# Chunk-sparse attention and softplus MLP on one core: paired casting loads, a causal triangle on TensorE, wide zero matmuls and a new order

## The chip, the cores and the metric

The kernel runs on one core of one Trainium2 chip. The metric is the device time of one launch in microseconds. The kernel before takes 265.45 us (median of three runs, 265.19 to 266.56).

## The reference

Attention over 4 batches, 8 heads, 768 positions and head size 64, then a two-layer MLP with softplus. Each query may look at its 6 best chunks of 32 keys, ranked by an upper bound from the chunk's element-wise minimum and maximum of k; the causal mask goes on top.

```python
k_min, k_max = k_chunks.min(axis=3), k_chunks.max(axis=3)      # 24 chunks of 32 keys
ub = sum(maximum(q * k_min, q * k_max))                        # [B, H, S, 24], causal by chunk
top_chunks = argsort(ub)[..., -6:]
scores = where(chosen & (pos_q >= pos_k), q @ k.T / sqrt(64), -1e9)
x = (softmax(scores) @ v) -> [B*S, H*D]                        # 3072 x 512
out = softplus(x @ w_in) @ w_out                               # 512 -> 2048 -> 512
```

## The kernel before, in words

The work is cut into 12 blocks: 4 batches times 3 blocks of 256 queries. Block n has k = n mod 3; its queries see 2(k+1) key tiles of 128. The stages of a block are these.

- **Loads.** q, k and v come in as bf16. The general loader `load` (L339) issues two casting DMAs on POOL's queue for each tensor, one for each tile of 128 tokens; every run that they write is one head of one token, 64 bf16 numbers. They go to an `io` buffer (8 of them), v to a resident tile. k and q of block 0 take another way, `load_pairs` (L352): two uncast loads for each on SP's queue, in which a partition holds two neighbouring tokens, and a cast on ScalarE (`io<-xp`, L258).
- **Turning.** In blocks 0 to 2, TensorE transposes k and q (L471, four matmuls for each tile of 128 tokens) into a PSUM tile; from block 3 on, SP's DMA transposes do it (L475). DVE takes chunk maxima and minima (`kx`, L498 and L490), puts them into a block-diagonal `bd`, and ScalarE or DVE copies k into the resident tiles `ka`, `kb` and q into `qt`, `qa`.
- **Choice.** Relu parts of q (`qpos`, `qneg`, L547 to L551) times `bd` give the bounds (L570, L574). DVE finds the sixth largest for each row (L597) and writes a mask `mraw` (L612), which is transposed (L627, L633 on TensorE, L636 by DMA) and copied beside q (`qa<-ph`, `qt<-pt`, at the copy helper's lines L258 for ScalarE and L259 for DVE). The mask then acts through extra rows of the score matmul.
- **Scores and values.** L687 and L688 make the scores of a pair of key tiles in PSUM, ScalarE takes the exponential (L695), and on the last pair of key tiles POOL zeroes what lies above the diagonal (`affine_select`, L705, in every block). L717 multiplies with v, DVE divides (L727, L728), and the result is turned into `x` (L743 on TensorE in blocks 0 to 2, L732 by DMA later).
- **MLP.** L791 makes h in 8 groups of 8 matmuls for a block, ScalarE takes exp (L796) and log(1+e) (L801) into `g`, L816 makes y, and SP stores it (L827).

The order is written by a planner at build time. `make_plan` lists operations with a duration for each engine that may run it, buffers from small pools, and a due time (`key`); `Plan.run` places them one by one by due time and by the earliest time at which its model has engine, data and buffer free, and the instructions are then issued in that order on every engine. Its model of the two DMA queues is a few lines in `run`; due times come from the numbers in `PAR`. `keep_awake` then fills every gap of over about 0.1 us that the plan leaves on TensorE before 45 us with matmuls of zeros, 128 columns wide (L852).

Of the kernel before, what the change touches and what calls it, by code (L numbers as in the profile page):

```python
# [63 lines left out]

class Op:
    __slots__ = ("name", "alts", "fn", "deps", "gate", "after", "succ", "alloc", "touch", "key",
                 "rel", "packet", "port", "due", "wait", "eng", "start", "end", "done", "dma", "n", "at", "inst")


class Plan:  # L70
# [5 lines left out]
    def op(self, name, alts, fn, deps=(), alloc=(), touch=(), key=None, dma=None, gate=(), after=(), rel=0.0, packet=19.0, port=False):  # L76
        o = Op()
        o.rel, o.packet, o.port = round(rel), packet, port
# [50 lines left out]
    @staticmethod  # L129
    def home_at(pool, s, e):  # L130
        t = 0.0
        for q, x, dma in pool.ends[s]:
            t = max(t, x + (LANDED[e] if dma else 0 if q == e == "PE" else LAT[q].get(e, 150)))
        return t

    def run(self, par):
# [7 lines left out]
        for o in reversed(topo):  # L144
            dur = min(c for _, c in o.alts) + (2500 if o.dma else 160)
            o.due = min([o.key] + [s.due - dur for s in o.succ])
        free = {"PE": 3000.0, "ACT": 2300.0, "DVE": 1000.0, "POOL": 800.0, "SP": 800.0}
        ring, packet = {"SP": 0.0, "POOL": 0.0}, {"SP": 19.0, "POOL": 32.0}
# [3 lines left out]
        while ready:  # L152
# [26 lines left out]
            if o.dma:  # L179
                other = "SP" if e == "POOL" else "POOL"  # L180
                at = max(o.end + (650 if e == "SP" else 1150), ring[e], 2650.0)
                back, part = max(0.0, ring[other] - at), packet[other] / o.packet
                ring[e] = at + o.dma + min(o.dma * part, back)
                ring[other] += min(o.dma, back / part)
                packet[e] = o.packet
                o.done = ring[e] + (450 if o.packet < 100 else 1000)
                if e == "SP":
                    o.end = max(o.end, ring[e] - 3500)
            else:
                o.done = o.end  # L190
# [4 lines left out]
            for b in o.touch:  # L195
                b.left -= 1
                b.ends.append((e, o.done, bool(o.dma)))
# [14 lines left out]
def mm(n):  # L212
    return max(25.0, n / 2.4 + 2.5)
# [6 lines left out]
def dve(n, rate=1.0):  # L220
    return n / (0.96 * rate) + 66


PAR = dict(
    dmat=3,
    dmaT=450,
    narrow=1,
    l0=1,
    over="soy",
    maskD=3,  # L230
    awake=(1.06, 45.0, 5.7),
    first=(64.42, 64.23, 29.03, 95.39),
    loads=((87.43, 130.15, 71.7), 19.14, (76.86, 12.06, 15.17), 41.22),
    tol={"PE": 0, "ACT": 0, "DVE": 0, "POOL": 2358, "SP": 0},
    alt=636,
    ohd=(229.35, 150.58),
    a=(-46.8, -33.92, -31.03, -0.05, 17.1, 24.77, 54.71, 88.7, 133.12, 175.62, 173.66, 255.42, 297.45, 469.8),
    prep=((77.31, -48.97, -81.43, 46.38), (-8.14, 24.92, -67.86, -43.68), (53.78, -16.07, -58.0, 11.26), (25.03, -41.37, -16.45, 11.23)),
    av=(-0.8, 4.76),
    ot=(12.12, 10.86),  # L240
    hlag=(8.7, 27.7, 34.1, -3.53, 34.9, 33.84, 33.54, 32.2, 25.36, -32.32, 54.03, 77.81),
    ylag=(7.32, 7.87, 25.64, 26.35, 28.67, 47.05, 47.88, 49.45, 10.02, 22.03, 47.36, 37.39),
    ahead=(3.4, 19.67, 10.64, 22.05, 12.72, 9.33, 70.63, 47.4, 103.95),
    sizes=dict(s=2, h=2, y=1, o=1, t=2, xf=2, xp=4, kT=2, io=8, kx=2, q=2, pn=2, ub=2, pt=4, osb=4, x=4, g=2, e=4, ysb=4, mT=2),
# [3 lines left out]
def make_plan(T, par):  # L248
# [19 lines left out]
    P.op("zero", [("DVE", 80)], lambda e: nc.vector.memset(T.zero, 0.0), key=-100000)  # L268
# [26 lines left out]
    chunk_rows = [P.op("c4", [("POOL", 900)], f4, [r4], key=3000)]  # L295
    mr0, bd0, kb0, vone, ohk = [], [], [], [], {}
# [11 lines left out]
    for k0, k1 in ((0, 1), (1, NBLK)):  # L308
        for h in range(2):
            o = P.op("ohk", [("SP", 450)], lambda e, k0=k0, k1=k1, h=h: rows_of(0, k0, k1, h), oh[k0:k1],  # L310
                     key=par["ohd"][k0] * 1e3, dma=300 * (k1 - k0))
# [636 lines left out]
```

## Time and profile before

| | |
|---|---|
| median of 3 runs | 265.45 us (265.19 to 266.56) |
| the profiled execution | 266.59 us, of which the span of its instructions is 264.8 us |
| TensorE busy | 255.0 us (96%), 2750 matmuls recorded |
| ScalarE, DVE, POOL busy | 211.0 us (80%), 142.5 us (54%), 110.8 us (42%) |
| DMA moved | 29.87 MB, 113 GB/s over the span |
| granted clock of TensorE, mean | 0.994 |

The busy share of TensorE holds the zero matmuls (22.7 us), and the ends of matmuls are modelled, so it has to be read with the timeline: what counts is when real matmuls start one right behind the other.

### The profile page before, as it was taken

How to read it: one execution, taken by the hardware profiler on the slowest of the kernel's cores; microseconds unless marked ns; L12 is line 12 of the kernel's file. 1: busy time of each engine (PE TensorE's matmuls, PEld its weight loads, DVE VectorE, ACT ScalarE, POOL GpSimd, SP SyncE). 2: the span in 40 equal slices, each digit the busy share in tenths (PEclk: the TensorE clock that was granted, in tenths of full speed). 3: DMA queues.
4: the chain of work that ended last, by engine and by line, in shares of the span. 5: the costliest groups of instructions: out<-in, count | busy, mean ns of one | idle time of the engine just before them, and what ended most of it. 6: DMA issues, size and time to landing. Idle time of an engine off the chain costs nothing.

```text
span 264.8 us, 7039 instructions
## 1 busy us (share of the span) xinstructions
PE 255.0 (96%) x2750; PEld 197.2 (74%) x2779; DVE 142.5 (54%) x500; ACT 211.0 (80%) x372; POOL 110.8 (42%) x193
## 2 busy tenths in 40 slices
PE   8698999999999999999999999999999999999995
PEld 8698898768775677788678864777888756887744
DVE  6589961019789667447634596584582164221012
ACT  3589999988687879999687992699997885999900
POOL 8927878798318520543990263401110211310000
PEclk9799999999999999999999999999999999999999
DMA  7996999999999984699699969624440123001022
GB/s 162 161 189 90 181 196 231 155 139 190 149 136 173 132 119 89 115 129 100 73 173 150 117 88 174 173 54 120 45 82 0 42 72 99 10 2 42 0 79 79
DMA packets 114719, 29.87 MB, mean 113 GB/s; under 512 B 104544, under 2 KB 111712, under 8 KB 114688
## 3 DMA queue, kind: packets, MB, share of 16 engines
q0 software_dynamic: 74944, 13.11, 66.5%
q1 hardware_dynamic: 39744, 16.33, 33.0%
q8 instruction: 21, 0.34, 0.6%
q14 instruction: 10, 0.08, 0.1%
HBM read 27.26 MB, written 6.29 MB: 127 GB/s over the span
## 4 chain that ended last, share of the span: by engine, by line
PE 86%; DMA 5%; DVE 3%; ACT 3%; issue 1%; POOL 0%; DVEq 0%; POOLq 0%
PE ph L791 30%; PE py L816 17%; PE pt L816 9%; PE po L717 7%; PE ps L687 5%; PE py L852 4%; PE ps L688 4%; DMA io<-in_k_dram 3%; DMA x<-osb 3%; PE pt L687 2%; PE pt L688 1%; PE pt L570 1%; ACT g L801 1%; PE ph L816 1%; ACT e L796 1%
## 5 line engine op out<-in xcount | busy, mean ns | idle before, releaser
L791 PE MATMUL ph<-x,w_in_sb 128*128 128x256 bf16 x768 | 91.8, 272 | 0.0
L705 POOL TENSOR_SCALAR_AFFINE_SELECT pt<-pt 128x256 bf16<-128x256 bf16 x96 | 39.5, 419 | 112.6 <-ACT pt L695 112.1
L791 PEld LDWEIGHTS <-w_in_sb 128*128 128x128 bf16 x768 | 73.6, 98 | 11.5 <-DMA w_in_sb<-in_moe_w_in_dram 0.5
L695 ACT ACTIVATE pt<-ps 128x512 bf16<-128x512 f32 (+1 forms) x134 | 69.9, 564 | 9.4 <-PE ps L688 8.8
L796 ACT ACTIVATE e<-ph 128x512 f32<-128x512 f32 x96 | 56.3, 606 | 12.5 <-PE ph L791 11.8
L816 PEld LDWEIGHTS <-g 128*128 128x128 bf16 x400 | 37.4, 98 | 31.4 <-ACT g L801 0.5
L816 PE MATMUL py<-w_out_sb,g 128*128 128x512 bf16 x231 | 57.8, 379 | 1.5 <-ACT ysb L258 0.2
L801 ACT ACTIVATE g<-e 128x1024 bf16<-128x1024 f32 x48 | 51.1, 1072 | 1.0
L695 ACT ACTIVATE pt<-pt 128x512 bf16<-128x512 f32 (+1 forms) x58 | 32.4, 584 | 0.6 <-PE pt L688 0.6
L717 PEld LDWEIGHTS <-pt 128*128 128x128 bf16 x672 | 26.8, 97 | 5.1 <-issue 0.6
L259 DVE COPY ysb<-py 128x512 f32<-128x512 f32 x12 | 8.3, 691 | 36.9 <-PE py L816 36.9
L717 PE MATMUL po<-v,pt 128*128 128x65 bf16 x610 | 26.4, 193 | 0.3 <-DVE osb L728 0.3
L816 PE MATMUL pt<-w_out_sb,g 128*128 128x512 bf16 x108 | 26.2, 379 | 0.2
L727 DVE RECIPROCAL rec<-po 128x4 f32<-128x4 f32 x43 | 7.6, 178 | 34.9 <-PE po L717 34.6
L490 DVE TENSOR_REDUCE kx<-kT 128x32 bf16<-128x1024 bf16 x18 | 21.0, 1209 | 8.9 <-DMA kT<-io 8.9
L852 PE MATMUL py<-zero 128*128 128x128 bf16 x243 | 22.7, 245 | 1.1 <-DVE zero L268 1.1
L339 POOL DMA_DIRECT2D v<-in_v_dram x24 | 21.6, 905 | 3.8 <-DMA io<-in_q_dram 1.5
L339 POOL DMA_DIRECT2D io<-in_k_dram x22 | 20.0, 910 | 5.7 <-DMA w_in_sb<-in_moe_w_in_dram 2.2
L339 POOL DMA_DIRECT2D io<-in_q_dram x22 | 19.9, 910 | 0.7 <-PE ph L791 0.6
L728 DVE TENSOR_TENSOR osb<-po,rec 128x256 bf16<-128x256 f32 x43 | 18.2, 424 | 2.7 <-DMA x<-osb 1.3
L852 PEld LDWEIGHTS <-zero 128*128 128x128 bf16 x243 | 18.3, 111 | 1.3 <-DVE zero L268 1.1
L687 PE MATMUL ps<-qa,ka 96*128 96x256 bf16 x71 | 18.3, 273 | 0.7 <-DVE qa L259 0.7
(99 smaller groups left out, 302.5 us busy)
## 6 DMA issues: line engine op xcount, KB each, us to landing
out_dram<-ysb SPq DMA_DIRECT2D x23, 256.0 KB, 2.4
v<-in_v_dram POOLq DMA_DIRECT2D x24, 128.0 KB, 7.6
io<-in_k_dram POOLq DMA_DIRECT2D x22, 128.0 KB, 7.2
io<-in_q_dram POOLq DMA_DIRECT2D x22, 128.0 KB, 7.1
w_out_sb<-in_moe_w_out_dram POOLq DMA_DIRECT2D x4, 512.0 KB, 8.0
w_in_sb<-in_moe_w_in_dram POOLq DMA_DIRECT2D x4, 512.0 KB, 9.6
xp<-in_k_dram SPq DMA_DIRECT2D x2, 256.0 KB, 3.2
xp<-in_q_dram SPq DMA_DIRECT2D x2, 256.0 KB, 6.3
```

Of the source, the lines that this page charges most:

```text
L339: lambda e, t=t: nc.gpsimd.dma_start(out=into(nm, n, t), in_=rows(nm, n, t)),
L490: nc.vector.tensor_reduce(kx.ap[:, :, j].rearrange("d p (t c) -> d t p c", t=NT), kT.ap.rearrange("d p x -> d (p x)").rearrange("d (t p c ...
L687: nc.tensor.matmul(sp.ap[:, 0:QB], kk[0:nr, p, j * 128:(j + 1) * 128], qq, start=True, stop=True)
L695: lambda e, sp=sp, pt=pt, h=h, j=j, w=w: nc.scalar.activation(pt.ap[:, h, j:j + 2].rearrange("k j c -> k (j c)")[:, 0:w], sp.ap[:, 0:w], A ...
L705: nc.gpsimd.affine_select(out=d, in_=d, compare_op=ALU.is_ge, fill=0.0, base=0, channel_multiplier=-1, pattern=[[0, 2], [1, 128]])
L717: nc.tensor.matmul(o[:, u, h], pt.ap[:, h, j, c0:c0 + 128], T.V[i][:, j, 2 * p + h, :], start=(j == 0), stop=(j == t0 + u))
L728: nc.vector.tensor_tensor(osb.ap[0], o[:, :, :, 0:D], osb.ap[1].to_broadcast([128, NT, 2, D]), op=ALU.mult)
L791: nc.tensor.matmul(o[:, j], T.w_in[:, dt, ft * 128:(ft + 1) * 128], x.ap[:, dt], start=(dt == 0), stop=(dt == KDM - 1))
L796: lambda e, hb=hb, eb=eb, f2=f2: nc.scalar.activation(eb.ap[:, f2 * 512:(f2 + 1) * 512], hb.ap, ACT.Exp),
L801: lambda e, eb=eb, g=g, f4=f4: nc.scalar.activation(g.ap[:, f4 * 4:(f4 + 1) * 4].rearrange("f j c -> f (j c)"), eb.ap, ACT.Ln, bias=1.0),
L816: nc.tensor.matmul(yb.ap[:, 0:c1 - c0], g.ap[:, f, u * 128:(u + 1) * 128], T.w_out[:, f, c0:c1], start=(f == 0), stop=(f == KFF - 1))
L852: z.fn = lambda e: T.nc.tensor.matmul(T.pools["y"].homes[0][:, 0:128], T.zero, T.zero, start=True, stop=True)
```

## The change

1. `load_both`: q of block 0 and k, q of blocks 1 and 2 come in as one casting DMA each on POOL's queue, in which a partition holds two neighbouring tokens and every run that is written is 128 bf16 numbers, where before it was two DMAs with runs of 64 (and, for q of block 0, two uncast loads on SP's queue and two casts on ScalarE). Since a pair of tokens then lies between the heads, TensorE turns each head by itself: 16 transposes of 64 columns for a tensor in place of 8 of 128. k of block 0 stays as it was.
2. In blocks 0 to 2 the causal triangle is added to the scores by a matmul of the identity with a triangle of large negative numbers, two for each last pair of key tiles, and POOL's `affine_select` on the exponentials falls away there. From block 3 on it stays.
3. Zero matmuls are up to 512 columns wide.
4. The planner gets a finer model of the two DMA queues (`Rings`), other costs of transfers, other due times and an offset for each name of an operation (`tweak`), and other pool sizes: `io` 4 for 8, `kT` 3 for 2, `pt` 5 for 4, `osb` 3 for 4, `e` 3 for 4. So the order on every engine is new.

```diff
+    def both(x):
+        return x.rearrange("s t h d -> s (t h d)").rearrange("s (h t d) -> s h t d", h=H, t=NT)
+
+    def load_both(nm, n, when):
+        b, k = blocks[n]
+        SBt[nm, n] = Buf(pool["io"])
+        o = P.op(f"ld {nm}{n}", [("POOL", 900)], lambda e: nc.gpsimd.dma_start(
+            out=both(SBt[nm, n].ap), in_=src[nm][b, :, k * QB:(k + 1) * QB].rearrange("h (s t) d -> s h t d", t=NT)),
+                 key=1e3 * when, dma=1280, packet=20.0, land=SKEW, alloc=[SBt[nm, n]])
...
             def transposes(nm, buf, t, n=n, ps=ps, p0=p0, whole=whole):
                 o = t_of(buf)
                 for p in ps:
+                    if whole[nm]:
+                        for h in range(2):
+                            nc.tensor.transpose(o[h * 64:(h + 1) * 64, p - p0, t * 128:(t + 1) * 128],
+                                                both(SBt[nm, n].ap)[:, 2 * p + h, t], T.ident)
+                        continue
...
-                        nc.tensor.matmul(sp.ap[:, 0:QB], kk[0:nr, p, j * 128:(j + 1) * 128], qq, start=True, stop=True)
-                        nc.tensor.matmul(sp.ap[:, QB:w], kk[0:nr, p, (j + 1) * 128:(j + 2) * 128],
-                                         qq[:, 1] if last else qq, start=True, stop=True)
+                        add = last and tri
+                        for c0, c1, x in ((0, QB, qq), (QB, w, qq[:, 1] if last else qq)):
+                            jj = j + c0 // QB
+                            nc.tensor.matmul(sp.ap[:, c0:c1], kk[0:nr, p, jj * 128:(jj + 1) * 128], x, start=True, stop=not add)
+                            if add:
+                                nc.tensor.matmul(sp.ap[:, c0:c0 + 128], T.ident, T.tri, start=False, stop=True)
...
-                    if last:
+                    if last and not tri:
                         def f_a(e, pt=pt, h=h, t0=t0):
...
-    l0=1,
+    l0=2,
+    both=3,
+    tri=3,
...
-    sizes=dict(s=2, h=2, y=1, o=1, t=2, xf=2, xp=4, kT=2, io=8, kx=2, q=2, pn=2, ub=2, pt=4, osb=4, x=4, g=2, e=4, ysb=4, mT=2),
+    sizes=dict(s=2, h=2, y=1, o=1, t=2, xf=2, xp=4, kT=3, io=4, kx=2, q=2, pn=2, ub=2, pt=5, osb=3, x=4, g=2, e=3, ysb=4, mT=2),
...
-        while True:
-            c = 107 if t < 1e3 * par["awake"][2] else mm(128)
...
+        for w in (512, 128):
+            while True:
+                c = w / 1.2 if t < 1e3 * par["awake"][2] else mm(w)
+                if t + c > o.start - 60:
+                    break
...
+                z.fn = lambda e, w=w: T.nc.tensor.matmul(T.pools["y"].homes[0][:, 0:w], T.zero[:, 0:128], T.zero[:, 0:w],
+                                                         start=True, stop=True)
```

Counted in the built programs: the zero matmuls go from 243 (all 128 wide) to 49 (33 of 512 and 16 of 128); the transposes of k and q from 48 to 88; 48 triangle matmuls are new; the selects on POOL go from 96 to 72; POOL's loads of q and k from 44 to 41. All other matmuls are as many as before.

200 lines of the change are left out of this document (133 added, 67 removed).

## The prediction

> **What bounds the kernel now.** I read the page first, for who is busy when.
>
> ```profile
> span 264.8 us, 7039 instructions
> ...
> PE   8698999999999999999999999999999999999995
> ...
> ACT  3589999988687879999687992699997885999900
> ...
> PEclk9799999999999999999999999999999999999999
> ...
> L705 POOL TENSOR_SCALAR_AFFINE_SELECT pt<-pt 128x256 bf16<-128x256 bf16 x96 | 39.5, 419 | 112.6 <-ACT pt L695 112.1
> ```
>
> TensorE's digits say 90% and more nearly everywhere, but zeros count as busy. So next came the busy time by stretch, of the zero matmuls alone and of all, and TensorE's timeline for the first real matmul of an MLP.
>
> ```profile
> 0.00:10.00 10.00, 5.80 (x52) 5.36 (x53) 0.11 (x1) 1.00 1.28 161
> 10.00:20.00 10.00, 7.33 (x79) 5.76 (x78) 0.00 (x0) 0.83 1.79 180
> 20.00:30.00 10.00, 5.85 (x79) 4.68 (x78) 0.00 (x0) 1.00 0.93 119
> ```
> ```profile
> sum 225.50, PE 223.49 PEld 167.98 DVE 112.77 ACT 183.52 POOL 83.45; mean PE 55.87 PEld 42.00 DVE 28.19 ACT 45.88 POOL 20.86
> ```
> ```profile
> 36.06 1.03 PE L791 MATMUL ph<-x,w_in_sb 128*128 128x256 bf16 x8
> ```
>
> The first three rows (time, busy us of zeros, count, ..., clock, DMA) show TensorE mostly on zeros for 30 us. The sum row covers 36.0 to 261.5 us: busy 223.5 of 225.5. So there are two kernels: a start-up until the first h at 36.06 us, bound by a chain of handoffs, and a rest bound by TensorE's own work. For that work I take start-to-start times from the chain of waits.
>
> ```profile
> 2.08 7.38 DMA io<-in_k_dram
> ...
> 10.12 2.22 PE py L852 x23
> ...
> 19.25 0.78 PE py L852 x14
> ...
> 43.19 2.62 PE ph L791 x24
> ...
> 60.33 0.66 PE po L717 x22
> ...
> 73.14 0.86 PE py L816 x4
> ```
>
> That is 109 ns for a matmul 256 wide, 215 for 512, 30 for 65 (values), 56 for 128 (14 in 0.78). Times the counts, with 26 ns for the small bounds matmuls (an estimate below the 30), the real matmuls are 234.2 us before and 239.1 after; the difference is 40 more transposes and 48 triangles, 88 x 56 ns = 4.9 us. In the instruction orders 11.5 us of that stand ahead of the first h before, 11.4 after. So before, 222.7 us of work after the first h take 225.5 us: 2.8 us are lost there, all the rest in the start-up.
>
> **What the change adds.** On TensorE 227.7 us are left after the first h instead of 222.7: 5.0 us dearer, on the path. Everything then hangs on how much sooner the first h comes. The zeros cost nothing while real work waits for its inputs: 33 wide and 16 narrow ones at 215 and 56 ns are 8.0 us, against 13.6 for 243 narrow ones; where one runs over, the next real matmul is late by 0.2 us at most.
>
> **The start-up, step by step.** Rows of ScalarE, DVE and POOL:
>
> ```profile
> 4.72 0.62 ACT L258 CAST io<-xp 128x512 bf16<-128x512 f32 x1 [0.26 <-DMA xp<-in_k_dram]
> ...
> 10.16 0.59 ACT L258 COPY qt<-ph 128x512 bf16<-128x512 bf16 x1 [0.80 <-PE ph L471]
> 10.64 0.62 ACT L258 CAST io<-xp 128x512 bf16<-128x512 f32 x1
> ...
> 16.30 1.06 ACT L547 ACTIVATE qpos<-qt 128x1024 bf16<-128x1024 bf16 x1
> 17.41 0.57 ACT L258 COPY qa<-ph 32x512 bf16<-32x512 bf16 x1
> ...
> 21.44 0.87 ACT L695 ACTIVATE pt<-ps 128x384 bf16<-128x384 f32 x2
> 22.20 1.00 ACT L258 COPY ka<-pt 64x1024 bf16<-64x1024 bf16 x1
> ...
> 27.09 0.50 ACT L695 ACTIVATE pt<-ps 128x384 bf16<-128x384 f32 x1
> ...
> 29.13 5.62 ACT L695 ACTIVATE pt<-ps 128x512 bf16<-128x512 f32 x11
> 34.64 0.64 ACT L258 COPY x<-pt 128x256 bf16<-128x256 bf16 x2
> ```
> ```profile
> 5.33 2.48 DVE L498 TENSOR_REDUCE kx<-pt 128x16 bf16<-128x512 bf16 x4 [0.80 <-PE pt L471]
> 7.73 1.17 DVE L259 COPY bd<-kx 64x32 bf16<-64x32 bf16 x2
> ...
> 10.98 0.66 DVE L549 TENSOR_SCALAR qneg<-qt 128x512 bf16<-128x512 bf16 x1
> 11.56 0.34 DVE L259 COPY bd<-kx 64x32 bf16<-64x32 bf16 x2
> ...
> 16.43 1.21 DVE L498 TENSOR_REDUCE kx<-ph 128x32 bf16<-128x1024 bf16 x1
> ...
> 31.84 0.42 DVE L728 TENSOR_TENSOR osb<-po,rec 128x256 bf16<-128x256 f32 x1
> ```
> ```profile
> DMA packets 3638, 0.47 MB, mean 156 GB/s; under 512 B 3616, under 2 KB 3638, under 8 KB 3638
> ```
> ```profile
> DMA packets 1135, 1.13 MB, mean 188 GB/s; under 512 B 33, under 2 KB 1135, under 8 KB 1135
> ```
>
> *q of block 0.* No row shows a casting load with runs of 256 B. Its rate lies between the loads with runs of 128 B alone (first row above, 8 to 11 us, 156 GB/s) and the weights, runs of 1 KB (second, 32 to 38 us, 188 GB/s): 256 KB take 1.4 to 1.7 us; I take 1.4 for its size beside 1.7 for two loads now, 0.3 us a tensor. It is POOL's first DMA, at about 1.7 us. The first pair of loads there, issued at 2.08, took 7.38 us to reach TensorE, beside four loads on SP's queue; two of those go. If nothing is saved it lands at 1.7 + 7.38 = 9.1; with half the traffic beside it and a shorter transfer I take 7.4 or before, all the same to TensorE, which is busy until 7.4: k's second cast ends at 5.34, and behind it stand transposes and zeros of 22 x 128 columns, 2.1 us at 2.22/23 = 97 ns each. So the load is hidden; if it lands at 9.1, all below is 1.7 us later. ScalarE is rid of two casts of 0.62, POOL's queue of one issue a tensor, and q of block 0 now stands ahead of k of block 1 there, which moves k's transposes behind q's.
>
> The Trainium skill (DMA: Bandwidth & Descriptors, Anatomy of one DMA) gives each DMA about 2 us fixed plus its bytes at 436 GB/s; by that a merged load saves 2 us a tensor, 10 us for five. The trace disagrees for queued loads: two in a row stream at 156 GB/s without such a gap. The sum keeps 0.3.
>
> *Mask of block 0.* 16 transposes of q take 0.9 us (7.4 to 8.3), two copies of 0.59 each to 9.5. DVE reduces k (2.48) with four `bd` copies between (1.17 and 0.34) until 9.3, then two `qa` copies and four relus, six at 0.5 (between `bd`'s 0.17 and 0.66), to 12.3; bounds, maxima and compares, 0.7 by small DVE pieces of 0.17, to 13.0. TensorE has 16 transposes of k of block 1 queued before the mask's transposes: to 13.9. The first mask copy starts at 14.1, against 17.41 before. The 3.3 us come from q's second half, which before was cast only at 10.64 and turned behind other work, and from half the clock: 23 zeros took 2.22 us where 14 later took 0.78.
>
> *Exponentials.* From that copy to the last exponential of block 0, ScalarE has, by the new order, four mask copies of 0.57 and two of like size, a relu of 1.06, k's two copies of 1.00, eight exponentials of 0.44 and a small copy of 0.33: 10.4 us, to 24.5. Before, the same point is 27.59. Lead 3.1 us. The new wait, scores for `tri`, is made on POOL behind the loads of q, k, v and one of w_out by about 14; the first scores come at 15.6, and if `tri` were late the whole chain would be.
>
> *First h.* Before, the way from 27.6 to 36.06 went over the selects on POOL, eleven exponentials of block 1 (29.13 to 34.75) and then ScalarE's copies of `x` at 34.64. The 24 selects of blocks 0 to 2 go, 0.42 us each, and values wait for ScalarE alone; nothing on POOL now holds up loads behind a select there. After: values 0.3, division 0.6, a reduction of k of block 2 ahead on DVE 1.21, the transposes and a copy 0.5: 27.2, and TensorE's order lets it through at 27.4. Weights: w_in's first quarter is in the first 2.5 MB on POOL's queue, 13 to 16 us of transfer from 4 us on at the two rates, landed by 24. Lead 8.7 us.
>
> *After it.* 27.4 + 227.7 + the same 2.8 lost = 257.9 against 261.5: gain 3.6 us. ScalarE must keep up: from 24.5 its order holds 28 exponentials at 0.51 (5.62 for 11), 11 of L796 of the same size, five of L801 at 1.0 like a copy of as many columns and 1.7 of copies, 26.6 us to 51.1; TensorE's 23.6 us to the values that wait for them end at 51.0 too. Level, so some of each will wait for the other; I leave the loss as it was and take **3.5 us**. The profiled execution took 266.6, 1.8 us outside its 264.8 span; it stands 1.1 above the median, from which I subtract: 265.45 - 3.5 = 262.0. Own range 260 to 264.
>
> **Rivals.**
>
> *More: the added 5 us hide (chance 0.14).* If ScalarE, not TensorE, sets the pace to 50 us, 32 of the triangles and 16 transposes of block 2 cost nothing there and 2.7 us come on top: about 259.3. For: ScalarE's 9s from 20 to 50 us. Against: the level sums above.
>
> *Nothing left (0.15).* The lead is eaten in start-up. q landing at 9.1 costs 1.7. And TensorE has nothing queued between q of block 1 (10.3) and the bounds (11.5 to 12.8): the clock may halve again, as in the row with 0.83, adding 0.9 us, as for those 23 zeros (2.22 against 1.28), to twice that. With 1.7 each, 262.0 + 3.4 = 265.4. The Trainium skill (TensorE: Matmul & The Clock Gate, The HAM clock gate) says that a window of 3.4 us with too little activity halves the clock for the next: the trace agrees, with the clock below 1 only right behind the wait for k that ended at 9.46. By that rule fewer zeros speak against this change.
>
> *Slower: POOL's queue in the long stage (0.21).* With 4 `io` buffers, loads of k and q run two blocks ahead instead of four, and each waits in POOL's queue for a DMA transpose to free its buffer. The selects of blocks 3 and up stand behind it, and values behind those.
>
> ```profile
> io<-in_k_dram POOLq DMA_DIRECT2D x22, 128.0 KB, 7.2
> ...
> kT<-io SPq DMA_TRANSPOSE x9, 8.5
> ```
>
> A load and its transpose take 7.2 + 8.5 = 15.7 us; a block is 225.5 / 11 = 20.5 us, so two blocks cover it 2.6 times. It decides once the lead shrinks below one block. Where it does, I price a pair of selects late by its own length, 0.84 us: in all nine blocks 7.6 us, 269.6; in half of them 265.8. Against: POOL waited 112 us for ScalarE at the selects and has 24 fewer.
>
> That the loads do not get wider runs is worth 5 x 0.3 us and off the path.
>
> **How the numbers follow.** The forecast has 0.50. Faster by over 0.5% (1.3 us, about what these runs can tell from no change) is 0.50 + 0.14 = 0.64, within 0.15, slower 0.21. The range for 8 times in 10 goes from 259.3 to 268: it leaves out half of the second case and the worse part of the slower one.
>
> **What would show it.** Right: the first L791 at 26 to 29 us; the first mask copy near 14; ScalarE's last exponential of block 0 near 24.5; TensorE busy 99% from there on; no clock below 1 after 10 us. Wrong: a first h after 32 us, or waits of TensorE for DVE or POOL beyond 60 us that sum to over 4 us.

## The result, and the profile after

The changed kernel takes 269.35 us (median of four runs, 269.07 to 270.43); the kernel before, beside it, 265.32 us (four runs, 264.95 to 266.56). The ratio is 1.0151, 95% interval 1.0107 to 1.0195: 1.5% slower, where 262.0 us was forecast and 268.0 was the end of the range. The profiled execution took 269.07 us, 1.8 more than its span. (The ratios leave out executions more than 1.5% above the fastest of the same kernel, and of e1_dve, e5_all and a_notri the profiled execution is such a one, at a mean clock of 0.986, 0.976 and 0.968.)

The page of the kernel after: the span, TensorE's digits and its clock, and the chain that ended last, by engine and by line.

```profile
span 267.3 us, 6777 instructions
...
PE   8798999989998899999989999999999999999994
...
PEclk9999999999999999999999999999999999999999
...
PE 62%; DMA 21%; ACT 9%; DVE 4%; issue 1%; POOL 1%; SPq 0%; POOLq 0%; DVEq 0%; ACTq 0%
```

The start-up is shorter and the row of the clock has no 7 in it, but 8s now stand in the middle, and DMA has a fifth of the chain (5% before). Two pieces of TensorE's timeline give the ends of the accounting (start, duration):

```profile
26.93 1.03 PE L891 MATMUL ph<-x,w_in_sb 128*128 128x256 bf16 x8
...
260.25 3.66 PE L916 MATMUL ph<-w_out_sb,g 128*128 128x256 bf16 x32
```

The first h comes at 26.93 us (forecast 27.4, before 36.06) and TensorE ends at 263.91 (before 261.55). With the counted 227.7 us of work behind the first h, 263.91 - 26.93 - 227.7 = 9.3 us are lost there, against 2.8 before. So: lead 9.1, added work 5.0, added loss 6.5, and TensorE ends 2.4 us later. The medians are 4.0 us apart because the profiled execution of before stands 1.3 us above its median and that of after 0.3 below: 2.4 + 1.3 + 0.3. A part of the lead belongs to these executions: before ran at half clock from 10.2 to 13.7 us (mean clock 0.994) and after did not. Among the 13 executions of before beside e1_dve, the four at 0.99 to 0.995 have a median span of 264.4 us and the eight above 0.997 one of 263.1, so of the 9.1 us some 1.3 (an estimate from these spans) fall away where before keeps its clock.

Where the loss lies shows in the busy time of TensorE by stretch (stretch, length, busy us and matmul records, clock, DMA share, GB/s). The kernel before:

```profile
36.06:50.00 13.94, 13.88 (x158) 1.00 1.60 205
50.00:80.00 30.00, 29.79 (x314) 1.00 2.03 154
80.00:110.00 30.00, 29.29 (x279) 1.00 1.05 119
110.00:140.00 30.00, 29.77 (x349) 1.00 1.39 127
140.00:261.50 121.50, 120.70 (x1184) 1.00 0.50 74
```

The kernel after:

```profile
26.93:50.00 23.07, 22.47 (x282) 1.00 1.65 187
50.00:80.00 30.00, 28.39 (x292) 1.00 2.05 168
80.00:110.00 30.00, 27.38 (x289) 1.00 1.09 128
110.00:140.00 30.00, 28.66 (x317) 1.00 1.02 109
140.00:263.90 123.90, 123.03 (x1195) 1.00 0.47 68
```

From 50 to 140 us TensorE is idle for 1.61 + 2.62 + 1.34 = 5.57 us, against 0.21 + 0.71 + 0.23 = 1.15 before. All idle time behind the first h is 7.04 against 2.01. The other 1.5 us of the added loss do not show as gaps: the profile gives a matmul of 256 columns 272 ns where the next can start after 109, so short waits lie under the modelled ends. One of the gaps, in DVE's timeline (in brackets: its idle time before, and what ended that):

```profile
52.96 1.22 DVE L586 TENSOR_REDUCE kx<-kT 128x32 bf16<-128x1024 bf16 x1 [2.50 <-DMA kT<-io]
54.09 0.17 DVE L827 RECIPROCAL rec<-po 128x4 f32<-128x4 f32 x1
54.30 0.42 DVE L828 TENSOR_TENSOR osb<-po,rec 128x256 bf16<-128x256 f32 x1
```

DVE runs its queue in order. The reduction of k of block 4 stands ahead of the second of four divisions of block 2; it waits for its DMA transpose, the division waits behind it, and TensorE waits for the division. At 81.62 the same comes with a later k (the chain below). The waits of TensorE (what it waited for, us in all, times, longest) and those of DVE and POOL that lie behind them:

```profile
PE pt L843 <- DVE osb L828: 1.3, 1, 1.3
...
PE po L817 <- DVE osb L828: 1.0, 1, 1.0
...
PE ph L891 <- DMA x<-osb: 0.9, 1, 0.9
PE pt L666 <- DVE qpos L647: 0.6, 1, 0.6
```
```profile
DVE kx L586 <- DMA kT<-io: 6.9, 4, 2.5
DVE qpos L647 <- DMA qt<-io: 6.4, 4, 3.7
...
POOL io L406 <- DMA kT<-io: 10.1, 2, 6.2
```

The kernel before has the same wait of DVE, and a longer one:

```profile
DVE kx L490 <- DMA kT<-io: 8.9, 2, 7.4
```

Its DMA transposes of k took a median of 8.5 us from issue to landing, those of after 4.8. So the transposes did not become slower. Yet TensorE's waits behind the first h of before sum to 0.5 us in the profile's list: nothing that TensorE needed at once stood behind that wait.

The chain of waits goes the same way through the middle of the kernel:

```profile
25.23 17.11 DMA io<-in_k_dram
42.39 10.54 DMA kT<-io
52.96 1.22 DVE kx L586
...
74.22 7.38 DMA kT<-io
81.62 1.22 DVE kx L586
...
95.00 5.20 DMA qt<-io
```

So the trace of after names transposes of later blocks that hold in-order queues. Whether they came late for the new order, or the order has no room for them anywhere, or the parts of the change bring it with them, is what the experiments ask.

### The profile page after: what moved, and what is told of

Read it like the earlier page. It is cut to its first block, busy times and chain, and to the rows that moved or that the text cites. A ratio compares the mean times of both kernels' runs of the same rounds, so it can differ in the third digit from the quotient of the medians.

```text
span 267.3 us, 6777 instructions
## 1 busy us (share of the span) xinstructions
PE 252.5 (94%) x2640; PEld 187.1 (70%) x2673; DVE 141.2 (53%) x494; ACT 213.1 (80%) x377; POOL 98.2 (37%) x167
## 4 chain that ended last, share of the span: by engine, by line
PE 62%; DMA 21%; ACT 9%; DVE 4%; issue 1%; POOL 1%; SPq 0%; POOLq 0%; DVEq 0%; ACTq 0%
PE ph L891 23%; PE py L916 12%; PE pt L916 9%; DMA kT<-io 7%; DMA io<-in_k_dram 6%; PE ps L787 6%; PE po L817 5%; PE pt L787 4%; DMA qt<-io 4%; DMA io<-in_q_dram 3%; DMA x<-osb 2%; ACT pt L795 2%; ACT e L896 1%; DVE kx L586 1%; ACT qt L320 1%
## 5 line engine op out<-in xcount | busy, mean ns | idle before, releaser
L805 POOL TENSOR_SCALAR_AFFINE_SELECT pt<-pt 128x256 bf16<-128x256 bf16 x72 | 28.4, 413 | 107.0 <-ACT pt L795 106.9
L916 PE MATMUL py<-w_out_sb,g 128*128 128x512 bf16 x218 | 55.5, 379 | 1.2
L795 ACT ACTIVATE pt<-pt 128x384 bf16<-128x384 f32 (+1 forms) x59 | 32.2, 590 | 1.7 <-PE pt L787 1.7
L916 PE MATMUL pt<-w_out_sb,g 128*128 128x512 bf16 x120 | 29.3, 379 | 0.4
L787 PE MATMUL ps<-qa,ka 96*128 96x256 bf16 (+1 forms) x142 | 24.0, 259 | 0.2
L787 PE MATMUL ps<-qt,kb 128*128 128x256 bf16 x124 | 21.9, 259 | 0.7 <-ACT pt L795 0.4
L787 PEld LDWEIGHTS <-ka 96*128 96x128 bf16 x192 | 17.4, 98 | 5.8 <-issue 0.3
L406 POOL DMA_DIRECT2D io<-in_q_dram x18 | 16.2, 903 | 11.5 <-DMA kT<-io 6.2
L827 DVE RECIPROCAL rec<-po 128x4 f32<-128x4 f32 x40 | 7.2, 180 | 25.0 <-PE po L817 24.5
L406 POOL DMA_DIRECT2D io<-in_k_dram x18 | 16.6, 923 | 9.5 <-DMA kT<-io 3.9
L787 PEld LDWEIGHTS <-kb 128*128 128x128 bf16 x192 | 16.6, 97 | 3.6 <-issue 0.7
```

What stands on the lines that cost most here:

```text
L406: lambda e, t=t: nc.gpsimd.dma_start(out=into(nm, n, t), in_=rows(nm, n, t)),
L787: nc.tensor.matmul(sp.ap[:, c0:c1], kk[0:nr, p, jj * 128:(jj + 1) * 128], x, start=True, stop=not add)
L795: lambda e, sp=sp, pt=pt, h=h, j=j, w=w: nc.scalar.activation(pt.ap[:, h, j:j + 2].rearrange("k j c -> k (j c)")[:, 0:w], sp.ap[:, 0:w], A ...
L805: nc.gpsimd.affine_select(out=d, in_=d, compare_op=ALU.is_ge, fill=0.0, base=0, channel_multiplier=-1, pattern=[[0, 2], [1, 128]])
L827: nc.vector.reciprocal(osb.ap[1], o[:, :, :, D:D + 1])
L916: nc.tensor.matmul(yb.ap[:, 0:c1 - c0], g.ap[:, f, u * 128:(u + 1) * 128], T.w_out[:, f, c0:c1], start=(f == 0), stop=(f == KFF - 1))
```

## The experiments

All runs in one table. "Work" and "lost" are as above: counted matmul work behind the first h, and what the time from the first h to TensorE's end has beyond it (from the profiled execution). Ratios are against runs of the kernel before on the same chip.

| kernel | median us | ratio (95%) | first h | TensorE ends | work | lost |
|---|---|---|---|---|---|---|
| before | 265.32 | | 36.06 | 261.5 | 222.7 | 2.8 |
| after | 269.35 | 1.0151 (1.0107 to 1.0195) | 26.93 | 263.9 | 227.7 | 9.3 |
| p_tri | 266.87 | 1.0045 (1.0006 to 1.0083) | 36.40 | 263.4 | 223.8 | 3.2 |
| p_both | 268.21 | 1.0101 (1.0060 to 1.0141) | 37.14 | 263.0 | 222.7 | 3.1 |
| p_all | 269.47 | 1.0137 (1.0072 to 1.0201) | 38.90 | 265.8 | 223.7 | 3.2 |
| e1_dve | 274.75 | 1.0316 (1.0237 to 1.0395) | 26.33 | 271.8 | 227.7 | 17.8 |
| e2_io8 | 270.93 | 1.0225 (1.0164 to 1.0285) | 26.69 | 265.4 | 227.7 | 11.0 |
| e3_hyb | 268.18 | 1.0106 (1.0059 to 1.0153) | 26.25 | 263.4 | 227.7 | 9.4 |
| e4_k3 | 268.79 | 1.0139 (1.0094 to 1.0184) | 26.25 | 264.6 | 227.7 | 10.6 |
| e5_all | 278.68 | none | 26.32 | 275.7 | 227.7 | 21.6 |
| e6_mix | 268.03 | 1.0107 (1.0062 to 1.0152) | 29.62 | 262.2 | 227.7 | 4.8 |
| a_notri | 282.07 | none | 28.48 | 277.6 | 226.0 | 23.1 |
| x_after_w | 273.77 | 1.0323 (1.0244 to 1.0401) | 30.14 | 266.3 | 227.7 | 8.5 |
| x_hyb_w | 271.22 | 1.0186 (1.0095 to 1.0277) | 30.81 | 265.7 | 227.7 | 7.2 |
| e7_slack | 270.28 | 1.0183 (1.0091 to 1.0276) | 30.45 | 263.6 | 227.7 | 5.4 |
| e8_awake | 264.89 | 0.9973 (0.9938 to 1.0007) | 26.84 | 259.5 | 227.7 | 4.9 |
| e9_two | 265.21 | 0.9975 (0.9941 to 1.0008) | 27.40 | 258.6 | 227.3 | 3.9 |
| e10_more | 265.62 | 1.0014 (0.9981 to 1.0046) | 26.80 | 260.2 | 227.7 | 5.6 |
| e11_both | 265.94 | 1.0030 (0.9996 to 1.0065) | 26.69 | 259.7 | 227.3 | 5.8 |

The theories, in words: the loss comes from DVE's queue alone, standing behind reductions of later blocks (theory 1); or from the new late order as a whole, which has no room for real latencies (theory 2); or from transfers of the long stage that land late, since the start-up is 9 us shorter and the same bytes have to come (theory 3). Rival A, from the prediction: four `io` buffers hold the loads back. Rival B: the added work of the parts is all of it.

### One part at a time, in the old order (p_tri, p_both, p_all)

The kernel before, with its order kept instruction by instruction; only the instructions that a part removes go, and those that it adds stand in their place. p_tri has the triangle alone, p_both the single loads alone, p_all these two and the wide zeros.

```diff
+    order = [o for o in order if o.name not in ("af0", "af1", "af2")]                    # p_tri, p_all
+    order = [o for o in order if not (o.name in ("ld q0.0", "ld q0.1", "cast q0.0", "cast q0.1") or
+                                      o.name in ("ld k1.1", "ld q1.1", "ld k2.1", "ld q2.1"))]   # p_both, p_all
+    extra("ld q0", "POOL", 0.0, lambda e: T.load_both("q", 0))
```

> The kernel before with the triangle by matmul in blocks 0 to 2 alone, every other operation in its old place: 24 selects of GpSimd go, 48 matmuls of 128 columns come, 48 x 56 ns = 2.7 us. Theory 1 and Rival A: the selects of block 0 and 1 stood on the way to the first h (about 0.8 us for a pair and the handoffs); first h 1 to 2 us earlier, 2.7 us more work, of which 16 matmuls (0.9 us) lie ahead of it: 265.5 to 267. Rival B (the parts cost the time): 267 to 268.

> The kernel before with the single casting loads alone (q of block 0 as GpSimd's first DMA, k and q of blocks 1 and 2 where the first of their two loads stood), every other operation in its place. 40 more transposes, 2.2 us. With all three parts in the old order the first h came at 38.7 in place of 36.1 (TensorE waited 4.5 us at 6 us for k), and with the triangle alone at 36.4. If the loads are what delays it: first h at 38 to 39, 267.5 to 269.5. If the wide zeros are: first h at 36 to 36.5, 266.5 to 267.5.

> The kernel before with the three changed parts and none of the new order: every remaining operation keeps the place that it had; q of block 0 is loaded by one casting load that is GpSimd's first DMA, k and q of blocks 1 and 2 by one where the first of the two stood, the triangle is added by matmul in blocks 0 to 2 and the selects there go, and zeros are 512 columns wide. TensorE's work grows by 88 x 56 ns = 4.9 us. Theory 1 (the parts cost their work, and what the start-up gains is bound by the old order; the loss of 6 us is the new order's): 2.5 to 4 us earlier first h, 4.9 more behind it, no gaps of TensorE over 1 us after 50 us: 266 to 268. Rival A (pools and loads): the same, as this kernel has 8 buffers. Rival B (the parts themselves cost it): 269 or more.

Measured: the lost time stays at 3.1 to 3.2 us in all three. The triangle costs 0.45%, the single loads 1.0%, all of it 1.4%. The first h does not come sooner: 36.40 without the selects, 37.14 with single loads, 38.90 with all. In p_all the waits of TensorE begin with

```profile
PE ph L486 <- DMA io<-in_k_dram: 4.4, 1, 4.4
```

The load of k of block 1 is issued at 3.87 us instead of 2.08, because the load of q of block 0 now stands ahead of it on POOL's queue, and its transposes start at 10.71 instead of 9.50. (In p_both, with the same place for q, they start at 9.72; what else delays the first h there was not separated.) So no part opens the gaps of the long stage, and none by itself brings the lead of 9 us. The lead is there only with the new order of the start-up; that order without the new loads was not run.

### The triangle inside the new order (a_notri)

The kernel after, with selects on POOL again in blocks 0 to 2, each behind its exponential.

```diff
-                        add = last and tri
+                        add = False
-                    if last and not tri:
+                    if last:
```

> The changed kernel with the triangle of blocks 0 to 2 made by selects on GpSimd again, each behind its exponential; order and loads else unchanged. TensorE has 48 matmuls less, 2.7 us. If the order has no slack (theory 2), the 24 selects (0.42 us each), which stand between loads that wait for the weights, make values late and with them the first h: 269 to 272. If TensorE's work counted in full, 266.5 to 267.

Measured: 274.7 to 283.9 us, the first h at 28.48 (26.93 in after). The waits of TensorE:

```profile
PE po L820 <- POOL pt L805: 7.9, 11, 2.3
```

In the new order the selects stand on POOL's queue between loads that wait for room, and the values wait for them. The triangle by matmul, which does not bring the first h sooner in the old order, is needed in the new one.

### DVE's queue alone (e1_dve)

Six operations of later blocks (four reductions of k and two mask copies) go behind the divisions that waited for them.

```diff
+    order = behind(order, [(197, 451), (180, 485), (214, 496), (211, 506), (212, 506), (215, 506)])
```

> The changed kernel with six VectorE operations of later blocks put behind a division that they stood ahead of: one reduction of k of block 4 and one of block 3 behind a division of block 2 each, a reduction of k of block 5 behind the first division of block 3, the other reduction of block 5 and two mask copies of block 4 behind the second one. Nothing else moves. Theory 1 (a reduction that waits for a DMA transpose of a later block stands ahead of the division that TensorE waits for): the gaps of TensorE at 52.97 (1.51 us) and from 83.8 to 86.4 (0.34, 0.38 and 1.18) go, 3.4 us, and with them some of the lateness that SyncE's queue has from them at 95 to 100 (1.1): 265 to 266.5. Rival A (the loads come late because io has 4 buffers and not 8, VectorE's order only shows it): the masks of blocks 3 to 5 are then late by as much and the time stays within 0.7 of 269.4. Rival B (the added transposes and triangles on TensorE are all of it): 269.4, as the work is the same.

Measured: 274.75 us. The first gap, 1.51 us in after, is gone; but the moved operations are late for their own readers:

```profile
PE pt L666 <- DVE qpos L647: 4.0, 2, 3.6
...
PE po L817 <- POOL pt L805: 1.2, 1, 1.2
```

The gap moves from the division to the bounds of the later block and grows. So these six moves do not help: what DVE waits for comes too late for the readers of the later block as well. (The last row is POOL's queue: the load of q of block 5 waited there for a transpose of k, with a select behind it. It is the mechanism of the "slower" rival, at 1.2 us, in this kernel.)

### Buffers (e2_io8)

The order of after is kept; eight `io` buffers are dealt out in turn instead of four. (Here and in e4_k3 and e5_all block 8 uses other q values, since q of block 10 lands in its buffer first; the work is the same.)

```diff
+    for kind, size in {'io': 8}.items():
+        new, seen = Pool(size), []
...
+        for i, b in enumerate(seen):
+            b.pool, b.slot = new, i % size
```

> The changed kernel, every engine's order as it is, with 8 buffers for k and q (io) in place of 4. Rival A (late loads for want of buffers): GpSimd's waits for a transpose ahead of loads (3.93 us at 53.8 and 6.17 at 62.8) go, the transposes and reductions behind them come earlier, TensorE's gaps shrink: 264 to 266. Theory 1: the transpose that VectorE waits for at 50 to 53 is of a k that was loaded behind seven weight transfers (issued at 25.23, landed at 42.36), and those at 62 and 82 were issued by SyncE behind mask transposes and stores, so buffers change little: 268 to 269.6. Rival B: 269.4.

Measured: 270.93 us, lost 11.0. Twice the buffers win nothing: the 10.1 us that loads wait for transposes in after are gone from POOL's list of waits, and the lost time is not smaller. The rival with the buffers falls.

### Earlier loads and transposes (e4_k3, e5_all)

e4_k3: with eight buffers, the loads of v of block 2 and of k, q of block 3 go ahead of v and q of block 4 on POOL's queue, and no longer wait for the last weights. e5_all has this, e1_dve's moves, and on SP's queue the transposes of block 3 ahead of the first store, with three copies of constants behind it.

```diff
+    order = behind(order, 'ld k4.1', ['ld v2.0', 'ld v2.1', 'ld k3.0', 'ld k3.1', 'ld q3.0', 'ld q3.1', ...])
+    for o in order:
+        if o.name[:5] in ("ld k3", "ld q3", "ld v3"):
+            o.gate = []
...
+    for m, ns in ((196, [179, 185]), (1021, [46, 48, 47])):        # e5_all
```

> The changed kernel with 8 buffers for k and q, and on GpSimd's queue the loads of v of block 2 and of k and q of block 3 ahead of those of v and q of block 4 (they were issued from 41.2 to 49.0 us and come about 8 us earlier; their wait for the last weights is gone). All else keeps its order. Theory 3 (late loads of block 3): SyncE's transpose of k of block 3, issued at 56.2, moves to about 50, the masks of block 3 with it, and 2 to 4 us of the loss from 50 to 110 go: 265.5 to 267.5. Theory 2 (the order on VectorE, SyncE and GpSimd as a whole is too tight, one early load does not loosen it): within 1.5 us of the run with 8 buffers alone, 269.5 to 272.

> The kernel with the early loads of block 3 and 8 buffers, and with it the six moves on VectorE of the run before, and on SyncE the transposes of k and q of block 3 ahead of the first store, and the three copies of constants of batch 1 (192 KB each, ahead of the first transpose of k of block 4) behind it. Theory 3, each late item in turn hides the next (mending VectorE alone moved the stall to 100 us): with all three mended the first two stalls go: 263 to 266. Theory 2: more than these stand too late behind 70 us (transposes of q of block 5 at 95 us, x of block 6 at 131 us), 267 to 270.

e4_k3: 268.79 us, 0.6 less than after. SP's timeline of e4_k3 shows why so little comes of it:

```profile
50.22 1.30 SPq L571 DMA_TRANSPOSE kT<-io  x1
58.61 0.36 SPq L927 DMA_DIRECT2D out_dram<-ysb  x1
59.16 5.17 SPq L571 DMA_TRANSPOSE qt<-io  x2
```

The transpose of k of block 3 is issued at 50.22 instead of 56.16. That of q of the same block stands behind the store of block 0's output, in order, and still starts at 59.16. e5_all decides nothing on the theories, because it made a wait of its own:

```profile
PE pt L666 <- ACT qpos L643: 6.4, 1, 6.4
```

The load of q of block 4, moved back, held SP's queue for 6.9 us, and TensorE lost 6.4 us at once.

### The late order of before (e3_hyb, e6_mix)

e3_hyb has all parts of the change and its order for what its plan starts in the first 38 us; everything later is in the order of before, with before's pools. The order is written out as a list (operation, engine, start, buffers). e6_mix is the same with 31 groups of instructions moved after a model of the queues.

```diff
-    order = plan.run(PAR)
+    order = by_hand(plan, T.pools)
+ORDER = """
+1G800 23S800,xp0 0D1000 8D1160 2D1290 14G1320 25S1360,xp1 27G1650,io0 12D1990 ...
```

> All parts of the change, and its order for what it starts in the first 38 us of its plan; everything behind that stands in the order of the kernel before, with that kernel's numbers of buffers (io 8, pt 4, osb 4, e 4, kT 2). Both kernels' work and start-up are unchanged, only the late order is the old one. Theory 2 (the 6.7 us that TensorE loses more behind its first h, 15.7 against 9.0 by the recorded matmuls, come from the late half of the new order alone): the first h stays at 26 to 28 us, the loss returns to 9 to 10.5: 262 to 264. Theory 3 (they come from the earlier start: with the first h 9.3 us earlier the loads of blocks 3 to 5, which stand behind 4 MB of weights, are late for any order): the loss stays at 13 or more and the time at 267 to 270.

> The same mixture as the first of these runs, with 31 groups of operations moved by 0.1 to 10 us in the list from which each engine's order is made, so that a model of the queues with k and q transposes taking from 1.1 to 1.9 times as long gives 254 to 255 us to TensorE's end for all of them (the mixture without these moves 256 to 259, the changed kernel's order 254 to 279). Theory 2: robust order, early start: 1 to 2 us under the mixture: 260.5 to 262.5, which would be faster than both kernels. Theory 3: 266 to 269 as the mixture.

e3_hyb, TensorE by stretch:

```profile
50.00:80.00 30.00, 28.72 (x305) 0.95 1.93 146
80.00:110.00 30.00, 29.84 (x290) 1.00 0.91 116
110.00:140.00 30.00, 29.95 (x347) 1.00 1.22 118
```

From 80 to 140 us 0.21 us are idle, where after has 3.96: the loss there belongs to the late order, taken with its pools (`pt`, `osb`, `e` and `kT` as before too; of the pools only `io` was run by itself). But between 26 and 80 us 7.4 us are lost now, and its waits show a transfer:

```profile
PE po L817 <- DMA v<-in_v_dram: 2.0, 1, 2.0
```

The old late order, begun some 10 us sooner, meets loads that have not landed. The wait for v ends at 49.02, and behind it TensorE ran at half clock for 3.4 us (mean 0.95 from 50 to 80 us), which is part of the 7.4. e6_mix loses 4.8 us in all, but three copies of constants were late in its start-up (`PE ps L787` waited 1.7 us for `kb<-ohb`), the first h came at 29.6, and 268.03 is left.

### Without six of eight weight loads (x_after_w, x_hyb_w)

After and e3_hyb without the last three quarters of both weights; the matmuls read the first quarter four times.

```diff
+    gone = [o for o in order if o.name in ("w_in1", "w_in2", "w_in3", "w_out1", "w_out2", "w_out3")]
+    order = [o for o in order if o not in gone]
```

> The changed kernel without six of the eight weight loads (the last three quarters of each weight matrix, 3 MB on GpSimd's queue from 15 to 40 us); the matmuls read the first quarter four times, so the output is another one and TensorE's work the same. Everything else keeps its order. The loads of blocks 3 and 4 that stood behind the weights then come 10 us and more earlier. Theory 3 (the transfers, not the late order, are behind TensorE): the loss behind the first h falls from 9.3 us to 4 or less: 262.5 to 265. Theory 2 (the late order has no slack, whenever the data come): the stalls from 80 to 140 us stay, since they hang on divisions, stores and masks ahead of transposes: at most the first 2 to 3 us come back, 266 to 268.

> The mixture (new start-up, old late order) without the same six weight loads. It lost 7.4 us from 26 to 80 us and 1.8 from there on. Theory 3: what it lost before 80 us was waiting for transfers (v of block 2 at 46.6 for 2.2 us, k of block 3), and goes: 261.5 to 264, faster than the kernel before. Theory 2 alone: the seam between the two orders costs it (VectorE and ScalarE late at 42 and 49 us), 266.5 to 268.5.

x_after_w, TensorE by stretch:

```profile
50.00:80.00 30.00, 30.00 (x327) 1.00 1.16 113
80.00:110.00 30.00, 27.75 (x296) 1.00 1.19 135
110.00:140.00 30.00, 28.57 (x303) 1.00 1.07 114
```

With 3 MB less to load, the 1.61 us idle from 50 to 80 us are gone to nothing; the idle time from 80 to 140 is 3.68, nearly the 3.96 of after. By its recorded matmuls, which are complete here (they sum to the counted 227.7 us), x_after_w loses 1.0 us up to 80 us and 6.5 from 80 to 140. In x_hyb_w the loss up to 80 us falls from 7.4 to 3.8. So behind 80 us the late order loses by itself. That late transfers are the loss before 80 us fits, but is not shown by these two: their first h came at 30.1 and 30.8, which by itself leaves the loads 3 to 5 us more, and in all x_after_w still lost 8.5 us.

The times of both kernels say nothing, because TensorE waited 1.8 and 3.7 us for k of block 2 ahead of the first h. The trace shows what came in its way. The three copies of constants on SP's queue had stood behind the last weights; without these they start at 13 to 16 us instead of 38 to 41, beside the load of k issued at 13.0. From 18 to 22 us SP's queue moved 0.63 MB and POOL's 0.25 in x_after_w (0.61 and 0.26 in x_hyb_w), where in after it was 0.00 and 0.76.

### The late order made anew (e7_slack, e8_awake)

All parts, the change's start-up, and a late order re-made from that of before (with before's pools, and without the wait of block 3's loads for the last weights) with two durations from the traces put into the planner's model: the three 192 KB copies of constants on SP's queue take 1.7 us of transfer each, and SP's transfers start 0.85 us later. e8_awake differs in the places of the zero matmuls only, which stand where the change's own plan has them.

```diff
-1G800 23S800,xp0 0D1000 8D1160 2D1290 14G1320 25S1360,xp1 27G1650,io0 ... 24A5016,io2 ...
+(the list with the starts of the change's plan for the first 38 us, from which the gaps for zeros are taken)
```

> All parts of the change, its order up to 38 us (loads of blocks 3 and up excepted, whose wait for the last weights is gone), and behind that an order made anew from that of the kernel before with a model in which the three 192 KB copies of constants take 1.7 us each and a transfer on SyncE's queue starts 0.85 us later than the change's own plan has it, as the traces show; with it the model gives TensorE's end at 258.8, where it has 260.9 for the mixture (measured 263.2) and 261.8 for the changed kernel (263.7). Both theories: the stalls of both halves shrink; 265 to 267, under the mixture by 1 to 3 us. If transfers set the pace before 80 us for any order (theory 3), no better than 266.

> The order with slack behind 38 us (the third of the runs before), with the zero matmuls put where the change's own plan puts them. That run had 4.5 us of zeros in TensorE's queue between 20 and 30 us where the changed kernel has 0.4, which held its first h at 30.3 (26.7 there); behind the first h it lost 5.4 us. If the zeros were what held it, the first h comes at 26 to 27 and with the loss of 5.4 TensorE ends at 259 to 260.5: 264.5 to 266, level with the kernel before. If the transfers set the pace up to 80 us, what is won at the first h is lost again there: 266.5 to 268.5, as the mixture.

e7_slack lost only 5.4 us, but 4.5 us of zeros that its list put between 20 and 30 us held the first h until 30.45: 270.28. e8_awake is without that (12 runs; the kernel before 17): 264.89 us, ratio 0.9973, level with before and 4.5 us under the changed kernel, with the same parts. Its first h is at 26.84, and its stretches:

```profile
50.00:80.00 30.00, 29.71 (x308) 1.00 1.68 141
80.00:110.00 30.00, 29.49 (x312) 1.00 1.22 135
110.00:140.00 30.00, 29.14 (x312) 1.00 1.33 122
```

Idle from 50 to 140: 1.65 us, against 5.57. So the lead of the start-up can be kept with all parts of the change, and 4.4 of the 6.5 us of added loss went with the late order, its pools and that wait. These three were not taken apart.

### What is left of it (e9_two, e10_more, e11_both)

e9_two: e8_awake with k, q of block 2 as two loads each again (16 transposes fewer). e10_more: its list taken further with the same model. e11_both: both.

```diff
-        o = P.op(f"ld {nm}{n}", [("POOL", 900)], lambda e: nc.gpsimd.dma_start(
+        o = P.op(f"ld {nm}{n}", [("POOL", 900)], lambda e: [nc.gpsimd.dma_start(
+            out=into(nm, n, t), in_=rows(nm, n, t)) for t in range(NT)][-1] if n == 2 else nc.gpsimd.dma_start(
```

> The order with slack and early first h (264.9, against 266.0 for the kernel before in its run), with k and q of block 2 as two casting loads each, as before the change, one right behind the other in the same place; TensorE has 16 transposes less there, 0.9 us. If the single load of token pairs buys nothing in block 2, whose data wait for the weights around them anyway, the work counts: 263.5 to 264.5. If GpSimd's two issues more (0.9 us each) push the weights and the loads of block 3 back, 265 to 266.

> The order with slack taken further in the same model (k and q transposes of 1.6, 2.0 and 2.4 us of transfer time): 258.0 to TensorE's end where the model gave 258.8. If the model's order of slack is what the chip sees, 263.5 to 265; if the rest of the loss, 4.5 us by the recorded matmuls, is no longer waits that the model knows, 264.5 to 266.

> Both of the two kernels before together: if both add up, 262.5 to 264; otherwise between them.

Measured: 265.21, 265.62 and 265.94 us, all level with before by their intervals. The further gains of the model are not there on the chip. Of the lead of 9 us, 4.6 to 5.0 are the added work and 1.1 to 3.0 the added loss, and the rest (TensorE ends at 258.6 to 260.2 us in the profiled executions, against 261.55 in one of before that was itself 1.3 us above its median) is within the 0.5% that these runs can tell.

## Why the prediction was wrong, point by point

**The start-up: right in its times, wrong in what brings them.** ScalarE's timeline of after has

```profile
12.96 0.57 ACT L320 COPY qa<-pt 32x512 bf16<-32x512 bf16 x1
...
23.46 3.12 ACT L795 ACTIVATE pt<-ps 128x384 bf16<-128x384 f32 x6
```

The first mask copy stands at 12.96 (forecast 14.1), the eighth exponential ends at 23.46 + 3.12/6 = 24.0 (24.5), the first h is at 26.93 (27.4). q of block 0 cost TensorE a wait of 0.9 us. But the prediction drew the lead from the parts (selects gone, casts gone), and p_tri, p_both and p_all show that in the old order the parts bring none; a_notri shows 1.5 us for the triangle in the new order. The rest is the new start-up order with the new loads, which were not taken apart.

**The added work: right.** 4.9 us of transposes and triangles; p_all, which adds the same in the old order, ends 4.2 us later for TensorE, with its loss at 3.2.

**The step that failed: "the same 2.8 lost".** This term measured 9.3. It was carried over from an order that the diff replaces: 2.8 us was what the kernel before lost with its own order, found for its own latencies. The prediction quoted the row that should have priced it (a DMA transpose of k, 8.5 us from issue to landing) and used it for buffers on POOL's queue, but did not ask what stands behind each waiter for such a transpose on DVE's and SP's queues in the new order. The order listed by engine would have shown it: the reduction of k of block 4 ahead of a division of block 2, the store of block 0 ahead of a transpose of q of block 3. That row is of before, where it cost TensorE nothing; the new order lost more with transposes that landed sooner. Of the 7.4 us between 262.0 and 269.35, this term has 6.5, and the first h, 0.5 sooner than forecast, gives some of it back. The other 1.4 us are the step from the profiled execution to the median: the prediction took the 1.1 us of before for both kernels, and the profiled execution of after stood 0.3 below its median.

**The cause, as far as shown.** The late order with its pools: behind 80 us by e3_hyb and x_after_w, and over the whole by e8_awake, which keeps the parts and the start-up and loses 4.9. Up to 80 us the order meets transfers that land late for it; that these alone are the loss there is argued. That the planner's model of SP's transfers is what made the order tight fits, since the order re-made with two measured durations holds; but e8_awake changed more than those two numbers, so this was only argued too. The 2.1 us that e8_awake still loses more than before stay open.

**"Slower: POOL's queue".** The sign and the price (269.6) came out, the mechanism did not: that the number fits is luck. Loads did wait for transposes to free a buffer (10.1 us), yet TensorE's loads of weights for the values waited for POOL's selects by 2.2 us in all, and eight buffers won nothing:

```profile
L817 PEld LDWEIGHTS <-pt 128*128 128x128 bf16 x672 | 25.6, 97 | 6.4 <-POOL pt L805 2.2
```

**"More".** Refuted: the added work was not hidden anywhere.

**"Nothing left".** The halved clock, its half of the reason, did not come: behind its first zero matmul TensorE was idle for no longer than 0.9 us in the first 12 us, where before it was idle for 2.24 us ahead of k and then at half clock from 10.2 to 13.7. The rule of the Trainium skill (TensorE: Matmul & The Clock Gate, The HAM clock gate), a halved clock after a window of 3.4 us with too little activity, fits both traces; it did not speak against this change, since 49 zeros, 33 of them wide, filled TensorE's waits as well as 243 narrow ones (busy 16.7 of the first 20 us, 16.6 before). (The row of the clock says nothing of the first 6 us: a transpose took 107 ns there in both kernels, 56 later.) The other half, q landing late, cost 0.9 us and not 1.7.

**The merged load.** The sum took 0.3 us a tensor; the estimate from the fixed cost that the Trainium skill gives each DMA (DMA: Bandwidth & Descriptors, Anatomy of one DMA) was 2 us. p_both, with nothing but merged loads, has its first h 1.1 us later than before. The measurement agrees with neither gain; its load of k of block 1 was issued 1.5 us later, behind that of q.

The sign of failure that the prediction named (waits of TensorE for DVE or POOL beyond 60 us of over 4 us) is not what the trace shows either: the waits that it files so sum to 2.0 us, and the idle time is spread over many short ones, of which the stretches give the sum.

## What to carry to other kernels

A loss measured under one hand-planned order belongs to that order: when a diff re-plans, price it anew, by listing for each operation that waits for a DMA what stands behind it on its in-order queue, and comparing that slack with the landing times of the trace. A lead won at the start can be lost again at the first place where transfers were just in time; there the loads have to come sooner by the same amount. Try each part in the old order as well; here three runs separated so what the parts cost from what the order does. And when an operation is taken out to test a cause, look what else waited for it.

## What the runs showed of the hardware that was not expected

Landing times on SP's queue spread widely about the medians. The DMA issues of after (KB each, median us from issue to landing):

```profile
ka<-ohb SPq DMA_DIRECT2D x1, 192.0 KB, 6.9
...
kb<-ohb SPq DMA_DIRECT2D x1, 192.0 KB, 10.0
kT<-io SPq DMA_TRANSPOSE x9, 4.8
```

The nine transposes of k land between 3.1 and 10.5 us after issue. On POOL's queue a load seems to start only with fewer than eight others in flight, as its timeline in after has it (the waits in brackets):

```profile
20.11 0.74 POOL L464 DMA_DIRECT2D w_out_sb<-in_moe_w_out_dram  x1 [0.62 <-DMA io<-in_k_dram]
...
28.59 0.88 POOL L406 DMA_DIRECT2D v<-in_v_dram  x1 [2.49 <-DMA w_in_sb<-in_moe_w_in_dram]
```

These are its 16th and 20th DMA, and each waited for the one eight places ahead. Copies on SP's queue took half of the transfer time from loads on POOL's (66% and 66% of 16 engines' span from 18 to 22 us in x_after_w), and an earlier load of 256 KB landed 11.2 us after issue, against 6.7 in after. And a gap of 2 us can cost the clock too, in the long stage as in the start-up: in e3_hyb TensorE waited 2.0 us for v until 49.02, and its clock was 0.50 from 50 to 52 us.
